# Windowed attention and a squared-ReLU feed-forward on one core: the second chunk of attention in plain float32, in another order of chunks

## The chip, the cores and the metric

One core of one Trainium2 chip runs the whole program. The metric is the time of one execution on the device in microseconds. Before the change it is 781.77 us (median of three runs, 781.71 to 782.03). Engines go by the profile's names: PE is the matrix engine, PEld its weight loads, DVE the vector engine, ACT the scalar engine, POOL the third elementwise engine, SP the queue that issues nearly all transfers.

## What is computed

```python
def _attn_ref(q, k, v, n_sink, window):          # q, k, v: [4, 8, 768, 64] float32
    scores = matmul(q, k.T) / sqrt(64)
    keep = (key < n_sink) | ((0 <= query - key) & (query - key < window))   # 4 and 128
    scores = where(keep, scores, -1e9)
    a = exp(scores - max(scores))
    return matmul(a / (sum(a) + 1e-9), v)

def _moe_ref(x, w_in, w_out, s, b):              # x: [3072, 512], w_in: [512, 2048]
    r = maximum(x @ w_in, 0)
    return (s * r * r + b) @ w_out
```

Inputs and output are float32. A second, general path in the program runs only if the limits on `n_sink` and `window` don't hold; with these inputs it is not taken.

## The kernel before

The 3072 rows are worked in eight **chunks** of 384 rows (`CH`), two per batch: an even chunk is the first half of a batch, an odd one the second half. Chunk *c* first gets its attention, which leaves its output transposed as two tiles `k.x[0]` and `k.x[1]` (a value rounded to the matrix engine's short float32 form, fp32r, and the remainder). Then the feed-forward of chunk *c* runs: 16 fragments *f* of the hidden width, each with a first product `h` (`l1`, 12 matmuls of 384 columns, L521) and a second product `po` (`l2`, 9 matmuls of 512 columns, L539), 32 steps in all. Both operands are split in two fp32r parts and three of the four partial products are added.

While the feed-forward of chunk *c* runs, the attention of chunk *c*+1 is put between its steps: the loop at L670 takes the feed-forward's steps one by one and, in proportion, the attention's slots. So there is a stretch with attention of chunk 0 alone, then seven **stages** (feed-forward of one chunk beside attention of the next), then the last feed-forward alone. A scheduler moves instructions within that order, engine by engine.

**Attention as in chunks 1 to 7** (`attn_slots`, L386) is split too. Per head, `prep_head` (L262) rounds queries, keys and values on ACT and forms the remainders on DVE (`qs`, L272) and POOL (`kl`, L273; `vv`, L278). A unit is one block of 128 queries: `unit_a` makes scores of at most 272 columns with two matmuls (L293, L294), masks and takes the row maximum on DVE (L298), exponentiates on ACT (L304) and copies the first keys' weights into `psk` on POOL (L305). `unit_b` transposes on PE, copies on ACT (L321), forms the remainder on DVE (`hl`, L322). `unit_c` multiplies by the values (L354), and per pair of heads `unit_d` adds what comes from the first keys and divides by the sum.

**Attention of chunk 0** (`first_slots`, L416) is plain: one float32 matmul per unit over all keys up to the diagonal (128, 256 and 384 columns, L443), mask and maximum (L445), exponent (L449), then `fn` divides by the row's sum on DVE (L460), `fb` transposes on PE (L468) and copies on ACT (L472), `fc` multiplies by the values (L480) in float32 into a bank of its own for each head, and casts and subtracts 64 partitions of it (L482, L483).

**The weights** come as 64-bit numbers. `make_weight` (L189) turns one fragment into two fp32r parts: two steps on ACT (L198, L199), two on DVE (L200, L201), an addition on POOL (L203), a cast on ACT (L208) and a subtraction on DVE or POOL (L214). `before(f)` calls it ahead of each `l1` of the first stage alone; the first two fragments are made during chunk 0's attention.

At the end, each feed-forward's three blocks of 128 rows are scaled by ACT into a tile `ot` (L543) and stored (L636). In the last one, all three take the two buffers of the tag `hl`.

Of the kernel before, what the change touches and what calls it, by code (L numbers as in the profile page):

```python
# [6 lines left out]
F32 = mybir.dt.float32  # L7
# [8 lines left out]
P = 128  # L16
# [17 lines left out]
E0, LB0, LC0 = 8, 4, 6  # L34
LB, LC, LD, L2 = 2, 4, 1, 2
# [3 lines left out]
def tile_kernel(ctx, tc, qT, kT, k0, v, vsk, n_sink, window, w, s, b, out):  # L39
# [15 lines left out]
    m_all = first.tile([P, 6 * P], MDT, tag="m", name="m_all")  # L55
# [34 lines left out]
    nc.sync.dma_start(lim[:, 0, :], n_sink.partition_broadcast(P))  # L90
    nc.sync.dma_start(lim[:, 1, :], window.partition_broadcast(P))
# [324 lines left out]
    def first_slots():  # L416
        k = Chunk()

        q = [wk.tile([P, NCC, CH], F32, tag=f"x{i}", name=f"q0{i}") for i in range(2)]
        k.x = [wk.tile([P, NCC, CH], F32R, tag=f"x{i}", name=f"x{i}_0") for i in range(2)]  # L420
        kk = first.tile([P, NCC, CH], F32, tag="k0", name="k0")
        vv = first.tile([P, NCC, CH], F32, tag="v0", name="v0")
        cc, tt, zz, sms = {}, {}, {}, {}

        def load():
            nc.gpsimd.memset(q[0][D:], 0.0)
            nc.vector.memset(q[1][:D], 0.0)
            for ps_ in (slice(0, 1), slice(1, NCC)):
                for hh in range(2):
                    hs = slice(hh * D, (hh + 1) * D)  # L430
                    nc.sync.dma_start(q[hh][hs, ps_, :], qT[0, ps_, hs, :CH].rearrange("r e s -> e r s"))
                    if hh == 0:
                        nc.sync.dma_start(kk[:, ps_, :], k0[:, ps_, :])
                nc.sync.dma_start(vv[:, ps_, :].rearrange("p r (n e) -> p r n e", n=BLK),
                                  v[0, ps_, :, :BLK].rearrange("r p n h d -> p r n (h d)"))

        def fa(h, i):
            pr = h // 2
            n = (i + 1) * P
            u = h * BLK + i  # L440
            uu = slice(u, u + 1)
            sc = psO.tile([P, 512], F32, tag="po", name="sc0")
            nc.tensor.matmul(sc[:, :n], q[h % 2][:, pr, i * P:(i + 1) * P], kk[:, pr, :n], start=True, stop=True)  # L443
            sm = first.tile([P, CH], F32, name="sm0", tag="sm0", bufs=E0)
            nc.vector.tensor_tensor_reduce(out=sm[:, :n], in0=sc[:, :n], in1=m_full[i], scale=-0.125, scalar=BIG,  # L445
                                           op0=ALU.add, op1=ALU.min, accum_out=negm[:, uu])
            if i == 0:
                zz[h] = first.tile([P, 2, BLK], F32, name="z0", tag="z0", bufs=4)
            nc.scalar.activation(sm[:, :n], sm[:, :n], AF.Exp, bias=negm[:, uu], scale=-1.0, accum_out=zz[h][:, 0, i:i + 1])  # L449
            sms[(h, i)] = sm  # L450

        def fn(h, i):
# [6 lines left out]
            sm = sms[(h, i)]  # L459
            nc.vector.tensor_scalar(out=sm[:, :n], in0=sm[:, :n], scalar1=z[:, 0, i:i + 1], scalar2=None, op0=ALU.mult)  # L460

        def fb(h, i):
            sm = sms.pop((h, i))
            if i == 0:
                tt[h] = first.tile([P, 4, 2 * P], F32, tag="tt0", name="tt0", bufs=3)
# [5 lines left out]
            out = tt[h][:, t0:t0 + i + 1, c0:c0 + P]  # L471
            nc.scalar.copy(out, tp[:, :(i + 1) * P].rearrange("p (k c) -> p k c", c=P))  # L472

        def fc(h):
            pr, hs = h // 2, slice(h % 2 * D, (h % 2 + 1) * D)
            o = ps("o0")
            t = tt.pop(h).rearrange("p k c -> p (k c)")
            for kb in range(BLK):
                c0 = kb * 3 * P
                nc.tensor.matmul(o[:, kb * P:CH], vv[:, pr, kb * P:(kb + 1) * P], t[:, c0:c0 + (BLK - kb) * P],  # L480
                                 start=(kb == 0), stop=(kb == BLK - 1))
# [4 lines left out]
        n = len(units)  # L486

        def slot(t):
            def f():
                if t == 0:  # L490
                    load()
                    constants()
                    nc.sync.dma_start(sb[:, 0:1], s.partition_broadcast(P))
                    nc.sync.dma_start(sb[:, 1:2], b.partition_broadcast(P))
                if t < n:
                    fa(*units[t])
# [4 lines left out]
                if 0 <= t - LB0 < n:  # L501
                    fb(*units[t - LB0])
                if 0 <= t - LC0 < n and (t - LC0) % BLK == BLK - 1:
                    fc((t - LC0) // BLK)
            return f

        return k, [slot(t) for t in range(n + LC0)]


    def moe_steps(x, store, wk, before=None, last=False):  # L510
# [21 lines left out]
        def l2(f):  # L532
            gg = g.pop(f)
            for tb in range(BLK):
# [6 lines left out]
                if f == NF - 1:  # L541
                    ot = wk.tile([P, DM], F32, name="ot", **(dict(tag="hl", bufs=HLB) if last else dict(tag="ot")))
# [115 lines left out]
    k, slots = first_slots()  # L658
# [86 lines left out]
```

## Time and profile before

| what | us |
|---|---|
| time, median of three runs | 781.77 |
| the profiled execution's own time | 781.77 |
| its span, first to last instruction | 780.0 |
| attention of chunk 0, from the first mask to the first `h` | 7.8 to 49.4 |
| first stage: feed-forward of chunk 0 beside attention of chunk 1 | 49.4 to 177.6 |
| second stage: feed-forward of chunk 1 beside attention of chunk 2 | 177.6 to 264.05 |
| third stage: feed-forward of chunk 2 beside attention of chunk 3 | 264.05 to 353.4 |
| last feed-forward alone | 705.1 to 772.5 |
| busy in the whole span: PE, DVE, ACT, POOL | 735.3, 513.6, 495.5, 268.8 |

The span is 1.8 us shorter than the time of the same execution. A stage is taken from the first `h` of one feed-forward to the first `h` of the next, as the chain of waits shows them. The granted clock is given as a share of the full one, 2.4 GHz; half of it is 1.2 GHz.

### The profile page before, as it was taken

The numbers are of one execution on the slowest core, as the hardware profiler recorded it, in microseconds if no ns is written. First come the engines' busy times: TensorE is split into PE (matmuls) and PEld (weight loads), VectorE is DVE, ScalarE is ACT, GpSimd is POOL, SyncE is SP. The second block draws the span as 40 slices with busy tenths as digits, with TensorE's granted clock in tenths as the row PEclk, the third lists the DMA queues.
The fourth block names the chain that finished last, engine by engine and source line by source line (L and its number), as shares of the span: only waits on it lengthen the run. The fifth ranks groups of instructions, "written<-read, shape, count | busy, mean of one in ns | idle before, by whom it ended". The sixth has DMA issues, their size and how long they took to land.

```text
span 780.0 us, 12112 instructions
## 1 busy us (share of the span) xinstructions
PE 735.3 (94%) x4036; PEld 656.9 (84%) x4036; DVE 513.6 (66%) x1250; ACT 495.5 (64%) x1231; POOL 268.8 (34%) x411
## 2 busy tenths in 40 slices
PE   7977988699999999999999999999999999999996
PEld 4655776579999999899999999899989999899985
DVE  6879998985676467655676466665676466663231
ACT  4886977766666576656666576656666576643222
POOL 3057668652343233322243233332343233210000
PEclk9989999999999999999999999999999999999998
DMA  7636205212112212112112212112111212001001
GB/s 271 273 103 229 105 14 170 76 34 77 42 54 59 73 43 67 35 43 76 43 53 57 76 43 62 40 43 76 43 53 55 77 43 60 21 1 42 1 1 45
DMA packets 28118, 54.21 MB, mean 70 GB/s; under 512 B 3600, under 2 KB 16528, under 8 KB 26128
## 3 DMA queue, kind: packets, MB, share of 16 engines
q1 hardware_dynamic: 28048, 53.36, 21.3%
q8 instruction: 34, 0.56, 0.3%
q14 instruction: 36, 0.29, 0.1%
HBM read 47.06 MB, written 6.29 MB: 68 GB/s over the span
## 4 chain that ended last, share of the span: by engine, by line
PE 76%; DVE 8%; ACT 7%; issue 3%; POOL 3%; DMA 2%; SPq 1%; ACTq 0%; POOLq 0%; DVEq 0%
PE h L521 30%; PE po L539 30%; PE o L354 5%; PE sc L294 2%; PE sc L293 2%; PE tp L317 2%; PE tp L316 2%; ACT w L199 1%; DVE r L525 1%; DMA w<-in_w 1%; PE o L480 1%; POOL w L203 1%; DVE w L201 1%; DVE qs L272 1%; ACT sm L304 1%
## 5 line engine op out<-in xcount | busy, mean ns | idle before, releaser
L521 PE MATMUL h<-x,w 128*128 128x384 f32 x1536 | 299.5, 343 | 8.7 <-DVE hl L322 3.8
L539 PE MATMUL po<-w,g 128*128 128x512 f32 x1152 | 301.6, 403 | 5.7 <-ACT g L527 3.7
L521 PEld LDWEIGHTS h<-x,w 128*128 128x128 f32 x1536 | 269.7, 190 | 14.5 <-issue 4.0
L539 PEld LDWEIGHTS po<-w,g 128*128 128x128 f32 x1152 | 211.6, 191 | 47.7 <-ACT g L527 4.9
L524 ACT ACTIVATE r<-h 128x384 f32<-128x384 f32 x128 | 62.9, 491 | 103.9 <-PE h L521 96.9
L298 DVE CUSTOM_DVE_ANT_0 sm<-sc,msk 128x272 f32<-128x272 f32 (+1 forms) x168 | 70.2, 418 | 78.4 <-PE sc L294 55.9
L525 DVE SCALAR_TENSOR_TENSOR r<-r,sb 128x384 f32<-128x384 f32 x128 | 84.1, 657 | 54.1 <-ACT r L524 54.0
L528 DVE SCALAR_TENSOR_TENSOR g<-r,sb,g 128x384 fp32r<-128x384 f32 x128 | 85.5, 668 | 45.6 <-ACT g L527 43.5
L305 POOL COPY psk<-sm 128x48 f32<-128x48 f32 x168 | 52.2, 311 | 162.9 <-ACT sm L304 161.7
L304 ACT ACTIVATE sm<-sm,negm 128x272 f32<-128x272 f32 (+1 forms) x168 | 85.4, 508 | 23.3 <-DVE negm L298 22.3
L527 ACT ACTIVATE g<-r,sb 128x384 fp32r<-128x384 f32 x128 | 78.7, 614 | 33.2 <-DVE r L525 32.1
L273 POOL TENSOR_TENSOR kl<-kraw,kh 128x544 fp32r<-128x544 f32 (+1 forms) x56 | 74.9, 1337 | 56.8 <-ACT kh L271 55.5
L321 ACT CAST hl<-tp 128x256 fp32r<-128x256 f32 (+1 forms) x168 | 58.8, 352 | 26.4 <-PE tp L317 26.2
L354 PE MATMUL o<-hl,vv 128*128 128x256 f32 (+1 forms) x400 | 71.4, 295 | 1.1 <-DVE hl L322 0.8
L322 DVE TENSOR_TENSOR hl<-tp,hl 128x256 fp32r<-128x256 f32 (+1 forms) x168 | 66.8, 398 | 7.5 <-ACT hl L321 6.7
L278 POOL TENSOR_TENSOR vv<-vraw,vv 128x256 fp32r<-128x256 f32 (+1 forms) x56 | 41.9, 747 | 60.9 <-ACT vv L277 59.0
L354 PEld LDWEIGHTS o<-hl,vv 128*128 128x128 f32 x400 | 54.9, 190 | 2.7 <-DVE hl L322 1.1
L293 PE MATMUL sc<-kh,qs 128*128 128x272 f32 (+1 forms) x168 | 47.8, 284 | 5.8 <-DVE hl L322 4.7
L363 DVE TENSOR_TENSOR xm<-o,y 64x384 f32<-64x384 f32 x56 | 31.0, 553 | 31.5 <-ACT y L362 31.3
L294 PE MATMUL sc<-kl,qs 128*128 128x272 f32 (+1 forms) x168 | 48.5, 289 | 0.0
L203 POOL TENSOR_TENSOR w<-w 128x1024 int32<-128x1024 int32 (+1 forms) x17 | 32.6, 1921 | 42.4 <-DVE z L458 19.3
L317 PE MATMUL tp<-identr,sm 128*128 128x128 f32 x168 | 45.7, 272 | 0.0
(112 smaller groups left out, 852.0 us busy)
## 6 DMA issues: line engine op xcount, KB each, us to landing
w<-in_w SPq DMA_DIRECT2D x15, 1024.0 KB, 8.9
kraw<-in_kT SPq DMA_DIRECT2D x32, 272.0 KB, 2.7
out<-ot SPq DMA_DIRECT2D x24, 256.0 KB, 2.0
qraw<-in_qT SPq DMA_DIRECT2D x28, 192.0 KB, 2.4
kraw<-in_kT SPq DMA_DIRECT2D x24, 208.0 KB, 2.4
vraw<-in_v SPq DMA_DIRECT2D x16, 256.0 KB, 2.7
vraw<-in_v SPq DMA_DIRECT2D x12, 192.0 KB, 2.3
vsraw<-in_vsk SPq DMA_DIRECT2D x28, 64.0 KB, 1.8
```

Source lines behind the costliest of these rows:

```text
L273: nc.gpsimd.tensor_tensor(out=hd.kl[:, :kw], in0=hd.k[:, :kw], in1=hd.kh[:, :kw].bitcast(F32), op=ALU.subtract)
L293: nc.tensor.matmul(sc[:, :n], hd.qs[:, qs], hd.kh[:, c0:c0 + n], start=True, stop=False)
L294: nc.tensor.matmul(sc[:, :n], hd.qs[:, qs], hd.kl[:, c0:c0 + n], start=False, stop=True)
L298: nc.vector.tensor_tensor_reduce(out=sm[:, :n], in0=sc[:, :n], in1=m, scale=-0.125, scalar=BIG, op0=ALU.add, op1=ALU.min, accum_out=negm[: ...
L304: nc.scalar.activation(sm[:, :n], sm[:, :n], AF.Exp, bias=negm[:, uu], scale=-1.0, accum_out=pp.zz[:, i, hh:hh + 1])
L322: nc.vector.tensor_tensor(out=lo, in0=tp[:, a:z], in1=hi.bitcast(F32), op=ALU.subtract)
L354: nc.tensor.matmul(hd.o[:, q0:q0 + n * P], hd.vv[:, kb, :], hd.hl[:, t, c0 * P:(c0 + n) * P], start=(hd.n == 0), stop=(i == BLK - 1 and kb ...
L521: nc.tensor.matmul(h[:, :CH], weight[f][:, 0, wi, cc * P:(cc + 1) * P], x[xi][:, cc, :], start=(i == 0), stop=(i == 11))
L525: nc.vector.scalar_tensor_tensor(out=r, in0=r, scalar=s_ap, in1=r, op0=ALU.mult, op1=ALU.mult)
L527: nc.scalar.activation(gg[:, 0, :], r, AF.Identity, bias=b_ap, scale=1.0)
L528: nc.vector.scalar_tensor_tensor(out=gg[:, 1, :], in0=r, scalar=b_ap, in1=gg[:, 0, :].bitcast(F32), op0=ALU.add, op1=ALU.subtract)
L539: nc.tensor.matmul(po[tb], gg[:, gi, tsl], weight[f][:, 1, wi, :], start=(f == 0 and i == 0), stop=(f == NF - 1 and i == 2))
```

## The change

It does four things.

- The chunks are worked in the order 0, 2, 1, 3, 4, 5, 6, 7, and chunk 2 (the first half of batch 1) gets its attention from the plain path, now `plain_slots(c)`, which the first stage holds. For chunk 2 its tiles come from the common pool under tags of the split path; its scores take a bank of the pool `psA`; per pair of heads `load_pair` loads keys, and per head queries and values beside 64 partitions or columns of zeros, which POOL writes.
- In both plain chunks the values of a head stand beside zeros, so that both heads of a pair add up in one bank, and one cast and one subtraction over 128 partitions take the place of two over 64.
- In chunk 0 the values are loaded head by head (8 transfers where there were 2), two of these and the two limits from ACT's queue; the mask tile moves to another pool.
- In the last feed-forward the third `ot` takes a buffer of the tag `ot`, so that each of the three has one of its own.

```diff
+ORDER = 0, 2, 1, 3, 4, 5, 6, 7
...
-    nc.sync.dma_start(lim[:, 0, :], n_sink.partition_broadcast(P))
-    nc.sync.dma_start(lim[:, 1, :], window.partition_broadcast(P))
+    nc.scalar.dma_start(lim[:, 0, :], n_sink.partition_broadcast(P))
+    nc.scalar.dma_start(lim[:, 1, :], window.partition_broadcast(P))
...
+                for pr in range(rs.start, rs.stop):
+                    for hh in range(2):
+                        hs = slice(hh * D, (hh + 1) * D)
+                        (nc.scalar if pr == 0 else nc.sync).dma_start(v0[:, pr, :, hh, hs], v[0, pr, :, :BLK, hh, :])
+
+        def zeros():
+            for hh in range(2):
+                nc.gpsimd.memset(v0[:, :, :, hh, (1 - hh) * D:(2 - hh) * D], 0.0)
+
+        def load_pair(pr):
+            kt = wk.tile([P, 544], F32, tag="kh", name="k_p")
+            nc.sync.dma_start(kt[:, :CH], k0[bb, :, pr, :])
+            for hh in range(2):
+                h = 2 * pr + hh
+                own, other = halves(h)
+                kk[h] = kt
+                q[h] = wk.tile([P, CH], F32, tag="qs", name="q_p")
+                nc.gpsimd.memset(q[h][other], 0.0)
+                nc.sync.dma_start(q[h][own], qT[bb, pr, own, :CH])
+                vv[h] = wk.tile([P, 4, P], F32, tag="vv", name="v_p", bufs=VB)
+                nc.gpsimd.memset(vv[h][:, :BLK, other], 0.0)
+                nc.sync.dma_start(vv[h][:, :BLK, own], v[bb, pr, :, :BLK, hh, :])
...
         def fc(h):
-            pr, hs = h // 2, slice(h % 2 * D, (h % 2 + 1) * D)
-            o = ps("o0")
+            pr, hh = h // 2, h % 2
+            if hh == 0:
+                os_[pr] = ps("o0")
+            o = os_[pr]
...
-                                 start=(kb == 0), stop=(kb == BLK - 1))
-            nc.scalar.copy(k.x[0][hs, pr, :], o[hs, :CH])
-            nc.vector.tensor_tensor(out=k.x[1][hs, pr, :], in0=o[hs, :CH], in1=k.x[0][hs, pr, :].bitcast(F32), op=ALU.subtract)
+                                 start=(hh == 0 and kb == 0), stop=(hh == 1 and kb == BLK - 1))
+            if hh == 1:
+                nc.scalar.copy(k.x[0][:, pr, :], o[:, :CH])
+                nc.vector.tensor_tensor(out=k.x[1][:, pr, :], in0=o[:, :CH], in1=k.x[0][:, pr, :].bitcast(F32), op=ALU.subtract)
...
-                    ot = wk.tile([P, DM], F32, name="ot", **(dict(tag="hl", bufs=HLB) if last else dict(tag="ot")))
+                    ot = wk.tile([P, DM], F32, name="ot", **(dict(tag="hl", bufs=HLB) if last and tb < 2 else dict(tag="ot")))
...
-    for c in range(NC_):
-        steps = moe_steps(k.x, store_at(c), wk, before if c == 0 else None, c == NC_ - 1)
+    for j, c in enumerate(ORDER):
+        steps = moe_steps(k.x, store_at(c), wk, before if j == 0 else None, j == NC_ - 1)
...
-            k, slots = attn_slots(c + 1)
+            k, slots = (plain_slots if j == 0 else attn_slots)(ORDER[j + 1])
```

Three places show what the scheduler made of it. The first is DVE in the first stage, between two fragments of weights. Before, the masks of the split path (L298) and the remainders `hl` stand between the weight steps L200, L201 and L214:

```order
L201 SCALAR_TENSOR_TENSOR w_456<-w_456,wt 128x1024
L528 SCALAR_TENSOR_TENSOR g<-r,sb,g 128x384
L322 TENSOR_TENSOR hl<-tp,hl 128x256
L298 ISA sm,negm<-sc,msk 128x272
L298 ISA negm 128x1
L322 TENSOR_TENSOR hl<-tp,hl 128x256
L200 TENSOR_SCALAR wt<-w_458 128x1024
L298 ISA sm,negm<-sc,msk 128x272
L298 ISA negm 128x1
L201 SCALAR_TENSOR_TENSOR w_458<-w_458,wt 128x1024
```

Now, with weight steps at L201, L202 and L215, the three divisions of a head (L497, of `sm_p`) stand together:

```order
L201 TENSOR_SCALAR wt<-w_460 128x1024
L576 SCALAR_TENSOR_TENSOR g<-r,sb,g 128x384
L495 RECIPROCAL z_p<-z_p 128x3
L202 SCALAR_TENSOR_TENSOR w_458<-w_458,wt 128x1024
L497 TENSOR_SCALAR sm_p<-sm_p,z_p 128x128
L497 TENSOR_SCALAR sm_p<-sm_p,z_p 128x256
L497 TENSOR_SCALAR sm_p_636<-sm_p_636,z_p 128x384
L215 TENSOR_TENSOR w_680<-w_456,w_680 128x2x512
L202 SCALAR_TENSOR_TENSOR w_460<-w_460,wt 128x1024
L201 TENSOR_SCALAR wt<-w_613 128x1024
```

The remainders `qs` and `hl` are gone from there, and the divisions are new. The second place is POOL in the first stage. Before, remainders and copies of the split path stand between the weights' additions (L203):

```order
L203 TENSOR_TENSOR w_261<-w_261 128x1024 [waits DVE_49]
L278 TENSOR_TENSOR vv<-vraw,vv 128x4x64 [waits Activation_49]
L305 COPY psk_95<-sm 128x3x16 [waits Activation_49]
L203 TENSOR_TENSOR w_263<-w_263 128x1024 [waits DMAHW7_49,DVE_49]
L273 TENSOR_TENSOR kl<-kraw,kh 128x544 [waits DMAHW2_49,Activation_49]
L305 COPY psk_95<-sm 128x3x16 [waits Activation_49]
L214 TENSOR_TENSOR w_638<-w_263,w_638 128x2x512 [waits Activation_49]
```

Now zeros for queries and values (L463, L466) stand there, and they wait for PE, which still reads the buffer that they fill:

```order
L463 MEMSET q_p 64x384 [waits DMAHW2_49,PE_49,Pool_49]
L215 TENSOR_TENSOR w_604<-w_269,w_604 128x2x512 [waits Activation_49,Pool_49]
L204 TENSOR_TENSOR w_456<-w_456 128x1024 [waits DMAHW6_49,DVE_49]
L204 TENSOR_TENSOR w_458<-w_458 128x1024 [waits DMAHW7_49,DVE_49]
L204 TENSOR_TENSOR w_460<-w_460 128x1024 [waits DMAHW0_49,DVE_49]
L463 MEMSET q_p 64x384 [waits DMAHW4_49,PE_49]
L204 TENSOR_TENSOR w_613<-w_613 128x1024 [waits DMAHW2_49,DVE_49,Activation_49]
L466 MEMSET v_p 128x3x64 [waits DMAHW3_49,PE_49]
```

So the additions for weights now stand in one queue behind steps of PE. The third place is ACT in chunk 0, where the first step on a weight, which waits for its transfer, stood as the 12th instruction after the cast of `sel`:

```order
L449 ACTIVATE sm_185,z_172<-sm_185,negm 128x384
L449 ACTIVATE sm_199,z_201<-sm_199,negm 128x128
L472 COPY tt_179<-tp_203 128x3x128
L449 ACTIVATE sm_210,z_201<-sm_210,negm 128x256
L198 ACTIVATE w_257<-w_257 128x1024
L472 COPY tt_213<-tp_214 128x128
```

It is now the 23rd, behind the fifth head's first exponent and the copies of three heads:

```order
L512 COPY tt_221<-tp_249 128x3x128
L512 COPY tt_259<-tp_260 128x128
L512 COPY tt_259<-tp_281 128x2x128
L512 COPY tt_259<-tp_296 128x3x128
L199 ACTIVATE w_263<-w_263 128x1024
L487 ACTIVATE sm_303,z_294<-sm_303,negm 128x256
```

That moves eleven instructions of attention ahead of that wait.

## Rows read from the trace of the kernel before

**Rows 1.** Stretches: length, busy PE, PEld, DVE, ACT, POOL (count), clock, DMA share, GB/s

```profile
7.80:49.40 41.60, 31.90 (x140) 22.03 (x139) 30.74 (x111) 33.79 (x92) 8.40 (x13) 0.90 0.59 232
49.40:177.60 128.20, 104.20 (x519) 86.81 (x519) 119.34 (x196) 99.88 (x201) 86.02 (x76) 0.94 0.33 112
177.60:264.05 86.45, 85.97 (x494) 79.22 (x493) 55.60 (x148) 55.86 (x152) 27.99 (x53) 1.00 0.19 55
264.05:353.40 89.35, 89.02 (x517) 82.24 (x517) 57.57 (x148) 58.28 (x152) 29.65 (x53) 1.00 0.18 55
```

**Rows 2.** First stage, groups by line and shape: busy us, mean ns, idle before

```profile
L528 DVE SCALAR_TENSOR_TENSOR g<-r,sb,g 128x384 fp32r<-128x384 f32 x16 | 16.0, 997 | 1.1 <-ACT g L527 1.1
L525 DVE SCALAR_TENSOR_TENSOR r<-r,sb 128x384 f32<-128x384 f32 x16 | 14.5, 903 | 0.0
L272 DVE TENSOR_TENSOR qs<-qraw,qs 64x384 fp32r<-64x384 f32 x9 | 12.1, 1343 | 0.3
L298 DVE CUSTOM_DVE_ANT_0 sm<-sc,msk 128x272 f32<-128x272 f32 x24 | 10.4, 432 | 0.5 <-PE sc L294 0.3
L322 DVE TENSOR_TENSOR hl<-tp,hl 128x256 fp32r<-128x256 f32 x24 | 9.9, 414 | 0.1
...
L273 POOL TENSOR_TENSOR kl<-kraw,kh 128x544 fp32r<-128x544 f32 x7 | 13.7, 1955 | 4.1 <-ACT kh L271 4.0
L305 POOL COPY psk<-sm 128x48 f32<-128x48 f32 x24 | 13.3, 559 | 4.6 <-ACT sm L304 4.5
```

**Rows 3.** Second stage, groups by line and shape

```profile
L525 DVE SCALAR_TENSOR_TENSOR r<-r,sb 128x384 f32<-128x384 f32 x16 | 10.0, 626 | 4.0 <-ACT r L524 4.0
L528 DVE SCALAR_TENSOR_TENSOR g<-r,sb,g 128x384 fp32r<-128x384 f32 x16 | 9.9, 617 | 5.5 <-ACT g L527 4.9
```

**Rows 4.** The chain of waits: start, us, what; float32 in chunk 0, then feed-forward

```profile
27.32 1.30 PE o L480 x6
28.62 0.33 PE tp L468 x3
...
182.31 2.12 PE h L521 x12
184.79 2.11 PE po L539 x9
```

**Rows 5.** Chunk 0 (7.5 to 49.4), groups by line

```profile
L449 ACT ACTIVATE sm<-sm,negm 128x128 f32<-128x128 f32 (+2 forms) x24 | 12.2, 508 | 3.7 <-DVE negm L445 3.6
L460 DVE TENSOR_SCALAR sm<-sm,z 128x128 f32<-128x128 f32 (+2 forms) x24 | 9.4, 447 | 0.1
L445 DVE CUSTOM_DVE_ANT_0 sm<-sc,m_all 128x128 f32<-128x128 f32 (+2 forms) x24 | 9.3, 417 | 1.6 <-PE sc L443 1.5
L472 ACT COPY tt<-tp 128x128 f32<-128x128 f32 (+2 forms) x24 | 8.5, 370 | 2.9 <-PE tp L468 2.6
...
L483 DVE TENSOR_TENSOR x<-o,x 64x384 fp32r<-64x384 f32 x7 | 3.9, 551 | 0.1
L482 ACT CAST x<-o 64x384 fp32r<-64x384 f32 x7 | 3.3, 473 | 1.0 <-PE o L480 0.9
```

**Rows 6.** Timeline of the start: the one large fill by POOL

```profile
0.90 1.37 POOL L426 MEMSET q<- 64x1536 f32 x1
```

**Rows 7.** Timeline of chunk 0, DVE's divisions and POOL: start, us, engine, line

```profile
29.20 1.90 POOL L203 TENSOR_TENSOR w<-w 128x1024 int32<-128x1024 int32 x1 [19.27 <-DVE z L458]
...
29.42 2.35 DVE L460 TENSOR_SCALAR sm<-sm,z 128x128 f32<-128x128 f32 x3
...
33.11 0.86 DVE L460 TENSOR_SCALAR sm<-sm,z 128x128 f32<-128x128 f32 x3
```

**Rows 8.** Chunk 0's first weight: the chain of waits, then the timeline

```profile
7.80 8.88 DMA w<-in_w
...
16.70 1.10 ACT L198 ACTIVATE w<-w 128x1024 int32<-128x1024 uint32 x1 [2.94 <-DMA w<-in_w]
```

**Rows 9.** Timeline of the end, the third block's scaling

```profile
773.92 0.60 ACT L543 ACTIVATE ot<-po 128x512 f32<-128x512 f32 x1 [1.46 <-DMA out<-ot]
```

More of the change, by code (lines that the diff above doesn't have):

```diff
@@ L413, in attn_slots, with plain_slots, halves, load_all @@
         return k, [slot(t) for t in range(n + LC + LD)]
-    def first_slots():
+    def plain_slots(c):
         k = Chunk()
[L419 to L428, printed above, removed]
+        k.c, bb = c, c // 2
+        q, kk, vv, cc, tt, zz, os_ = {}, {}, {}, {}, {}, {}, {}
+        if c == 0:
+            q0 = [wk.tile([P, NCC, CH], F32, tag=f"x{i}", name=f"q0{i}") for i in range(2)]
+            k0_ = first.tile([P, NCC, CH], F32, tag="k0", name="k0")
+            v0 = first.tile([P, NCC, BLK, 2, P], F32, tag="v0", name="v0")
+            for h in range(H):
+                q[h] = q0[h % 2][:, h // 2, :]
+                kk[h] = k0_[:, h // 2, :]
+                vv[h] = v0[:, h // 2, :, h % 2, :]
+        k.x = [wk.tile([P, NCC, CH], F32R, tag=f"x{i}", name=f"x{i}_{c}") for i in range(2)]
+        def halves(h):
+            own, other = slice(0, D), slice(D, P)
+            return (own, other) if h % 2 == 0 else (other, own)
+        def load_all():
+            nc.gpsimd.memset(q0[0][D:], 0.0)
+            nc.vector.memset(q0[1][:D], 0.0)
+            for rs in (slice(0, 1), slice(1, NCC)):
@@ L437, in fa @@
         def fa(h, i):
-            pr = h // 2
             n = (i + 1) * P
-            u = h * BLK + i
+            u = (c * H + h) * BLK + i
             uu = slice(u, u + 1)
-            sc = psO.tile([P, 512], F32, tag="po", name="sc0")
-            nc.tensor.matmul(sc[:, :n], q[h % 2][:, pr, i * P:(i + 1) * P], kk[:, pr, :n], start=True, stop=True)
-            sm = first.tile([P, CH], F32, name="sm0", tag="sm0", bufs=E0)
+            sc = psO.tile([P, 512], F32, tag="po", name="sc0") if c == 0 else ps("sc0")
@@ L445, in fa @@
+            nc.tensor.matmul(sc[:, :n], q[h][:, i * P:(i + 1) * P], kk[h][:, :n], start=True, stop=True)
+            if c == 0:
+                sm = first.tile([P, CH], F32, name="sm0", tag="sm0", bufs=E0)
+            elif i < 2:
+                sm = wk.tile([P, W], F32, name="sm_p", tag="sm", bufs=SMB)
+            else:
+                sm = wk.tile([P, 544], F32, name="sm_p2", tag="kl")
             nc.vector.tensor_tensor_reduce(out=sm[:, :n], in0=sc[:, :n], in1=m_full[i], scale=-0.125, scalar=BIG,
@@ L500, in f @@
                         fn(t // BLK, i)
[L501 to L504, printed above, removed]
+                if 0 <= t - lb < n:
+                    fb(*units[t - lb])
+                if 0 <= t - lc < n and (t - lc) % BLK == BLK - 1:
+                    fc((t - lc) // BLK)
             return f
-        return k, [slot(t) for t in range(n + LC0)]
+        return k, [slot(t) for t in range(n + lc)]
     def moe_steps(x, store, wk, before=None, last=False):
```

47 lines of the change are left out of this document (27 added, 20 removed).

## The prediction

> **What bounds the kernel now.** I read the share of busy time first (PE 94% of the span), then cut the span at the places where one feed-forward's first `h` follows another's, and read the busy time of each engine per stretch [rows 1]. The reader is to see that the 94% hides two regimes. From 177.6 us on, PE is busy to within half a microsecond of each stage (85.97 of 86.45, 89.02 of 89.35) at the full clock: there only PE's work counts. In the first stage, 49.4 to 177.6, it is another engine: DVE is busy 119.34 of 128.20 us (93%), ACT 99.88, POOL 86.02, and PE's clock falls to 0.94 of full on average because PE waits. The same feed-forward beside the same kind of attention takes 89.35 us later, so this one stage holds some 39 us that PE does not need. Chunk 0's attention before it (41.6 us) is bound by no single engine: 31.9, 30.7 and 33.8 us on PE, DVE and ACT.
>
> Next I read the first stage by groups [rows 2]. DVE does three things there: the weights, the squares `r` and `g` (14.5 + 16.0 us), and the attention of chunk 1, of which `qs`, the masks and `hl` alone are 12.1 + 10.4 + 9.9 us. The same `r` and `g` cost 626 and 617 ns each in the second stage [rows 3] and 903 and 997 ns here; the difference goes with POOL, which is busy two thirds of this stage and one third of the next.
>
> **The first stage, PE's side.** Plain float32 costs PE more. Three products of 384, 256 and 128 columns (six records) took 1.30 us and three transposes 0.33 us back to back [rows 4]. A head needs two such sets of products and six transposes: 2 x 1.30 + 2 x 0.33 = 3.26 us, a chunk 8 x 3.26 = 26.1 us. The feed-forward is 16 x 2.12 + 16 x 2.11 = 67.7 us [rows 4]. So PE needs 93.8 us in the changed stage, where the split path beside the same feed-forward needed 89.35 [rows 1]: 4.4 us more work.
>
> **The first stage, DVE's side.** Off go the groups above (32.4 us) and some 17 us in smaller groups of the same attention, which I estimate by the second half's usual stage: it has 57.57 us of DVE in all [rows 1], less 16 x (0.626 + 0.617) = 19.9 for the squares, so attention is 37.7 even where POOL does not disturb, and the 12.1 us of `qs` here would there be about 5. I take 37.7 as the lower and 49 as the upper end. On come the plain groups as chunk 0 shows them: masks 9.3, divisions 9.4, subtractions 4 x 0.55 [rows 5], and about 5 us of the short steps of sums and maxima: 26 us. DVE then stands at 119.3 - 49 + 26 = 96 to 119.3 - 38 + 26 = 107 us if its other work stays as dear as now. It should not: POOL loses `kl` and `psk` (13.7 + 13.3 us [rows 2]) and more, and gets 16 fills of a quarter of the size that took 1.37 us [rows 6] or less, some 5 us. If the squares came down to their price of the second stage, that is 30.5 - 19.9 = 10.6 us less. So DVE lies between 85 and 107 us; with POOL's load about halved I take 93. ACT loses the roundings of queries, keys and values, keeps exponents (12.2) and copies of transposes (8.5 [rows 5]); from 99.9 it falls, and binds less than now.
>
> **Its length.** PE at 93.8 and DVE near 93 leave no cover for each other's waits. For how near a stage comes to its busiest engine there are two rows: 93% in this stage now, with one clear bound, and 33.79 of 41.60 = 81% in chunk 0, where three engines are level [rows 1]. So 93.8/0.93 = 101 to 93.8/0.81 = 116 us. I take 106.5 (88%), nearer the first, because the weights' chain, the order of the stage and its length are those of this stage. That is 128.2 - 106.5 = 21.7 us less (27 to 12).
>
> A rule speaks against this part. Three divisions of one head took 2.35 us beside an addition of POOL and 0.86 us without one [rows 7]; eight heads bring 24 of them into the stage where POOL adds the weights. The Trainium skill says in "SBUF — State Buffer", section "Who interferes with whom", that a DVE instruction of the copy or tensor-scalar kind can take both ports, one pair of which is POOL's, and that the later of the two then waits for the whole instruction of the other. By that rule every head could lose what this one lost, and the trace agrees in the one place shown. I price it from the rows: 8 x (2.35 - 0.86) = 12 us at most, if each head meets an addition. POOL will be busy about half the stage, so half of it, 6 us, is in the 93 above already; all of it makes a rival below.
>
> **The stage after.** The second stage now carries attention of chunk 1, a second half, instead of chunk 2, a first half. Both prices are in [rows 1]: 89.35 - 86.45 = 2.9 us dearer. All later stages keep their kinds. +2.9.
>
> **Chunk 0.** ACT's first step on a weight waited 2.94 us for its transfer, which took 8.88 us from its issue at 7.80 [rows 8]. In the new order eleven more instructions of attention stand ahead of it, over 4 us of work at 508 and 370 ns [rows 5], so the wait should be covered. Twelve issues stood ahead of that transfer on SP, which came at 7.80, so at most 0.65 us each; now fourteen do, so it lands up to 1.3 us later. Four casts and four subtractions go: 4 x 0.473 on ACT and 4 x 0.551 on DVE [rows 5]. POOL's two fills beside the values, 1.37 us together by [rows 6], find room, since it is busy 8.40 of the 41.6 us [rows 1]. Bounds: -4.5 us (wait and casts both gone) and +1.3 (the wait merely moves). I take -2.5.
>
> The values now come in pieces of 64 numbers, 256 bytes, where a pair's 128 numbers stood together. "DMA: Bandwidth & Descriptors", section "Specifications", of the Trainium skill says that pieces under 512 bytes don't reach full rate; no row here has such a transfer of this size. By it chunk 0's term would be nearer to 0 than to -2.5, an estimate.
>
> **The end.** The third block's scaling waited 1.46 us for the first block's store [rows 9]; its new buffer was last stored a stage earlier. The last store follows it directly: -1.5.
>
> **The sum** is made against the profiled execution's 781.77, which is also the median: -21.7 + 2.9 - 2.5 - 1.5 = -22.8, **759.0 us**. With all the ends: -27.3 + 2.9 - 4.5 - 1.5 = -30.4, 751.4; and -12.4 + 2.9 + 1.3 - 1.5 = -9.7, 772.1.
>
> **Rivals.**
> - *PE fills up at once.* If DVE falls to 85 us, PE alone binds as in the later stages: 93.8 plus some 3 us at the start, 97. -31.2 + 2.9 - 2.5 - 1.5 = -32.3: 749.5. For it: later stages lose half a microsecond. Against it: their DVE is at 57 us, not 85. Chance 0.10.
> - *DVE stays the bound.* The rule above: all heads meet POOL, DVE is at 93 + 6 = 99 to 107, at 88% of the stage 113 to 121; take 117. -11.2 + 2.9 - 2.5 - 1.5 = -12.3: 769.5. For it: 997 [rows 2] against 617 ns [rows 3]. Against it: POOL's smaller load. Chance 0.14.
> - *POOL closes a ring, and it gets slower.* Twelve of the sixteen fills wait until PE has read the buffer's last use, and the weights' additions stand behind them in the same queue; PE waits for those weights. Where PE reaches a fill's release just before it needs the next weight, the addition, the cast and the subtraction are on its path. One such passage is POOL 1.9 us [rows 7] and more for the cast and the remainder. From the forecast to no gain it takes 22.8/12 = 1.9 us at each fill, which is one addition per fill; all twelve with 2.1 us, a step of the feed-forward [rows 4], give 759 + 25 = 784. For it: the order puts fills directly ahead of additions. Against it: in the order the weights' additions stand two or three fragments ahead of PE. Chance 0.05, of which 0.04 ends slower.
> - That the change does not do what it says is excluded for its main part by the order: the divisions and no `qs` or `hl` stand in the first stage.
>
> **How the numbers follow.** My forecast has 0.70, the floor 0.10, DVE 0.14, the ring 0.05, and 0.01 is left for a stall in no row. The range 750 to 772 takes in the forecast's ends and the DVE rival and leaves out most of the floor and the ring: about 8 in 10. A change is told from none at 0.2%, 1.6 us. Faster is forecast, floor and DVE: 0.94. Slower is the ring's 0.04; the rest of the ring and the unknown stall are the same, 0.02.
>
> **What would show it.** The stretch from the first `h` to the second feed-forward's first `h` should be 101 to 116 us, with PE busy above 95% of it, the clock above 0.97 and `r` and `g` near 750 ns. The next stage should be 89.4 us. The first `h` should come at about 47 us, and ACT's wait for the first weight be under 1 us. The last scaling should wait for PE alone. I am wrong if DVE is still over 93% busy in the first stage, if PE waits there for POOL's products, or if the second stage is longer than 90 us.

## The result and the profile after

The changed kernel takes 776.38 us (median of 4 runs, 776.11 to 776.96), the kernel before 781.74 beside it (4 runs): a ratio of 0.9934, 95% interval 0.9920 to 0.9947. It is faster, but by 5.4 us and not by the 22.8 forecast, and it lies outside the range. The profiled execution took 776.96 us.

The same stretches as in [rows 1], for the changed kernel (length; busy PE, PEld, DVE, ACT, POOL; clock; DMA share; GB/s):

```profile
7.80:42.50 34.70, 26.47 (x135) 18.66 (x134) 29.32 (x116) 29.80 (x84) 6.43 (x13) 1.00 0.93 296
42.50:169.90 127.40, 105.32 (x488) 84.85 (x487) 103.67 (x173) 83.65 (x166) 52.00 (x38) 0.95 0.27 93
169.90:259.30 89.40, 89.10 (x518) 82.27 (x517) 57.60 (x148) 58.07 (x151) 29.79 (x52) 1.00 0.21 61
```

Chunk 0 is 6.9 us shorter (41.60 before), the second stage 2.95 longer, and the first stage, where 21.7 us were to go, lost 0.8. DVE did lose its work there (119.34 to 103.67) and POOL too (86.02 to 52.00). The time did not follow. The sum of the three, -6.9 - 0.8 + 2.95, is the change of the span, 780.0 to 775.2, to within 0.1 us.

The groups of that stage that answer to [rows 2] (line, operation, tiles, shapes, count | busy us, mean ns | idle before):

```profile
L573 DVE SCALAR_TENSOR_TENSOR r<-r,sb 128x384 f32<-128x384 f32 x16 | 19.9, 1241 | 4.3 <-ACT r L572 4.3
L576 DVE SCALAR_TENSOR_TENSOR g<-r,sb,g 128x384 fp32r<-128x384 f32 x16 | 12.7, 792 | 3.2 <-ACT g L575 3.1
L204 POOL TENSOR_TENSOR w<-w 128x1024 int32<-128x1024 int32 x11 | 24.1, 2196 | 32.8 <-DVE w L202 24.7 <-ACT tt_p L512 5.5 <-ACT sm_p L487 2.5
L497 DVE TENSOR_SCALAR sm_p<-sm_p,z_p 128x256 f32<-128x256 f32 x8 | 6.1, 761 | 0.0
L494 DVE TENSOR_SCALAR z_p<-z_p 128x3 f32<-128x3 f32 x8 | 5.5, 691 | 0.5 <-ACT sm_p L487 0.5
```

`r`, which was to fall from 903 to about 750 ns, rose to 1241. A step `z_p` on three columns takes 691 ns on average. The timeline shows why (start us, us, engine, line, operation):

```profile
70.24 2.28 POOL L204 TENSOR_TENSOR w<-w 128x1024 int32<-128x1024 int32 x1 [2.83 <-DVE w L202]
70.69 2.24 DVE L573 SCALAR_TENSOR_TENSOR r<-r,sb 128x384 f32<-128x384 f32 x1
...
75.73 0.62 DVE L573 SCALAR_TENSOR_TENSOR r<-r,sb 128x384 f32<-128x384 f32 x1
...
89.89 2.20 POOL L204 TENSOR_TENSOR w<-w 128x1024 int32<-128x1024 int32 x1 [1.16 <-DVE w L202]
90.26 1.86 DVE L494 TENSOR_SCALAR z_p<-z_p 128x3 f32<-128x3 f32 x1
```

The `r` that starts 0.45 us after a POOL addition ends 0.41 us after that addition does; the next one, alone, takes 0.62. The `z_p` ends 0.03 us after its addition.

Not every DVE step is held. The masks (L481) take scores from a bank that PE wrote, and one tile; one that ran at 78.72, inside the addition from 78.41 to 80.56, took its 0.41 us. The steps of `L202` or `L215` beside such an operation took up to 2.57 us, alone 1.2.

The same stage in pieces, in the columns of [rows 1]:

```profile
60.00:80.00 20.00, 15.89 (x77) 12.46 (x78) 20.00 (x36) 15.00 (x28) 7.93 (x5) 1.00 0.27 106
80.00:104.00 24.00, 18.95 (x83) 15.39 (x82) 23.85 (x33) 16.64 (x30) 11.82 (x9) 0.86 0.08 21
104.00:116.00 12.00, 8.54 (x41) 6.18 (x39) 9.07 (x10) 4.31 (x10) 7.38 (x5) 1.00 0.58 194
116.00:145.00 29.00, 23.57 (x118) 19.03 (x117) 26.10 (x59) 22.21 (x53) 11.37 (x11) 1.00 0.17 50
145.00:170.00 25.00, 24.38 (x115) 20.90 (x116) 9.94 (x22) 10.79 (x26) 4.48 (x5) 0.93 0.12 35
```

DVE's 81% of the stage is a mean of two parts. From 60 to 104 us it is busy 43.85 of 44 us and PE 34.84; from 145 us on, when the weights are made, PE is busy 24.38 of 25 and DVE 9.94.

### The profile page after: what moved, and what is told of

The parts are those of the page before. It is cut to its first block, busy times and chain, and to the rows that moved or that the text cites. A ratio compares the mean times of both kernels' runs of the same rounds, so it can differ in the third digit from the quotient of the medians.

```text
span 775.2 us, 11989 instructions
## 1 busy us (share of the span) xinstructions
PE 733.9 (95%) x4024; PEld 654.1 (84%) x4024; DVE 497.0 (64%) x1222; ACT 477.8 (62%) x1187; POOL 237.1 (31%) x377
## 4 chain that ended last, share of the span: by engine, by line
PE 78%; DVE 9%; ACT 3%; issue 2%; POOL 1%; DMA 1%; ACTq 0%; DVEq 0%; POOLq 0%
PE h L569 32%; PE po L587 30%; PE o L355 5%; PE sc L295 2%; PE sc L294 2%; PE tp L318 2%; DVE w L202 2%; PE tp L317 2%; DVE r L573 1%; DVE w L215 1%; DVE wt L201 1%; DVE sm_p L497 1%; DVE g L576 1%; PE o L522 1%; PE ts L368 1%
## 5 line engine op out<-in xcount | busy, mean ns | idle before, releaser
L572 ACT ACTIVATE r<-h 128x384 f32<-128x384 f32 x128 | 62.9, 492 | 114.3 <-PE h L569 110.2
L299 DVE CUSTOM_DVE_ANT_0 sm<-sc,msk 128x272 f32<-128x272 f32 (+1 forms) x144 | 60.8, 422 | 80.4 <-PE sc L295 65.6
L306 POOL COPY psk<-sm 128x48 f32<-128x48 f32 x144 | 38.3, 266 | 166.0 <-ACT sm L305 164.7
L305 ACT ACTIVATE sm<-sm,negm 128x272 f32<-128x272 f32 (+1 forms) x144 | 73.7, 512 | 20.4 <-DVE negm L299 19.2
L274 POOL TENSOR_TENSOR kl<-kraw,kh 128x544 fp32r<-128x544 f32 (+1 forms) x48 | 61.4, 1279 | 56.3 <-ACT kh L272 50.0
L322 ACT CAST hl<-tp 128x256 fp32r<-128x256 f32 (+1 forms) x144 | 51.3, 356 | 28.7 <-PE tp L318 28.2
L323 DVE TENSOR_TENSOR hl<-tp,hl 128x256 fp32r<-128x256 f32 (+1 forms) x144 | 57.9, 402 | 8.1 <-ACT hl L322 7.2
L355 PE MATMUL o<-hl,vv 128*128 128x256 f32 (+1 forms) x352 | 61.5, 293 | 0.0
L279 POOL TENSOR_TENSOR vv<-vraw,vv 128x256 fp32r<-128x256 f32 (+1 forms) x48 | 34.8, 724 | 59.8 <-ACT vv L278 57.4
L295 PE MATMUL sc<-kl,qs 128*128 128x272 f32 (+1 forms) x144 | 41.4, 287 | 0.0
L294 PE MATMUL sc<-kh,qs 128*128 128x272 f32 (+1 forms) x144 | 40.4, 281 | 0.0
```

The lines of the kernel that those rows point to most:

```text
L274: nc.gpsimd.tensor_tensor(out=hd.kl[:, :kw], in0=hd.k[:, :kw], in1=hd.kh[:, :kw].bitcast(F32), op=ALU.subtract)
L295: nc.tensor.matmul(sc[:, :n], hd.qs[:, qs], hd.kl[:, c0:c0 + n], start=False, stop=True)
L323: nc.vector.tensor_tensor(out=lo, in0=tp[:, a:z], in1=hi.bitcast(F32), op=ALU.subtract)
L355: nc.tensor.matmul(hd.o[:, q0:q0 + n * P], hd.vv[:, kb, :], hd.hl[:, t, c0 * P:(c0 + n) * P], start=(hd.n == 0), stop=(i == BLK - 1 and kb ...
L572: nc.scalar.activation(r, h[:, :CH], AF.Relu, scale=1.0 / WUP)
```

## Experiments

Theory 1: POOL's operations that read two tiles, the weights' additions above all, hold DVE off, and the weights' preparation keeps the first stage long. Rivals: late transfers of weights (2), POOL's fills that wait for PE ahead of its additions (3), attention left over behind the last weight (4). In each run I read where the second stage's first `h` comes: 177.6 us before, 169.9 after.

**The two parts apart.** The first keeps the new first chunk alone, the second the float32 half alone.

```diff
-ORDER = 0, 2, 1, 3, 4, 5, 6, 7
+ORDER = 0, 1, 2, 3, 4, 5, 6, 7
-            k, slots = (plain_slots if j == 0 else attn_slots)(ORDER[j + 1])
+            k, slots = attn_slots(ORDER[j + 1])
```

> The changed kernel with the old order of chunks and with the split attention in the first stage again: only the new first chunk and the buffers of the last stores are left of the change. If the whole gain of 5.4 us is the first chunk's (first h at 42.5 instead of 49.4 us) and the float32 half is worth nothing in the first stage (128.2 to 127.4) and costs 2.9 in the second, this kernel takes 781.7 - 6.9 = 774.8 us, 1.5 below the changed one. If instead the late first weight of the new first chunk (issued at 14.75 instead of 7.80 us) was paid for in the first stage, that stage is longer than 128.2 us here and the time is 777 to 782.

```diff
-            v0 = first.tile([P, NCC, BLK, 2, P], F32, tag="v0", name="v0")
+            v0 = first.tile([P, NCC, CH], F32, tag="v0", name="v0")
...
-            if hh == 0:
-                os_[pr] = ps("o0")
+            if hh == 0 or c == 0:
+                os_[pr] = ps("o0")
...
+            if c == 0:
+                hs = slice(hh * D, (hh + 1) * D)
+                nc.scalar.copy(k.x[0][hs, pr, :], o[hs, :CH])
```

> The changed kernel with the old first chunk (values of both heads in one tile, two accumulations a pair, small loads and the first weight as before): only the float32 half in the first stage is left. If the two parts add up, first h is back at 49.4, the first stage is 127.4 and the second 89.4 us, and the time is 776.4 + 6.9 = 783.3 us, slower than before by 1.5. If the new first chunk spoiled the first stage (late weights, the sub-512-byte pieces of its loads), the stage is 107 to 115 us here and the time 764 to 771.

The first chunk alone: 782.15 us, ratio 1.0005 (0.9994 to 1.0015), no gain. The float32 half alone: 779.23, ratio 0.9969 (0.9957 to 0.9981). The stretches of the first, then those of the second:

```profile
7.80:42.10 34.30, 26.04 (x132) 18.43 (x132) 29.31 (x115) 29.63 (x86) 6.13 (x11) 1.00 0.87 281
42.10:177.05 134.95, 106.72 (x526) 91.11 (x525) 122.04 (x197) 101.11 (x205) 88.58 (x77) 0.91 0.31 107
```

```profile
7.80:49.30 41.50, 31.35 (x140) 21.52 (x139) 30.89 (x113) 33.81 (x90) 5.68 (x10) 0.92 0.68 246
49.30:173.50 124.20, 105.78 (x484) 87.11 (x483) 103.35 (x173) 83.16 (x164) 51.26 (x38) 0.92 0.27 96
```

The first `h` came 7.3 us earlier in the first run, and the stage became 6.8 us longer: its end stayed (177.05 against 177.6). DVE's work over both stretches is 29.31 + 122.04 = 151.35 us, before 30.74 + 119.34 = 150.08. The time and the longer stage are what the expectation gave for a late first weight, but no step of ACT or DVE waited for a weight's transfer in either stretch. I read it so: with split attention DVE's work sets the end of the stage, wherever its first `h` lies. The float32 half alone brought the end forward by 4.1 us and paid 2.9 back in the second stage. Both together brought it forward by 7.7: with less work for DVE the earlier start is worth something.

**The stage without attention, and without POOL's additions.**

```diff
+        if c:
+            def fill():
+                for x in k.x:
+                    nc.gpsimd.memset(x.bitcast(F32), 0.0)
...
+            return k, [fill]
...
         return k, [slot(t) for t in range(n + lc)]
```

> The changed kernel with no attention at all in the first stage: the rows of chunk 2 are filled with zeros and not computed (its output rows are wrong by that much), so that the stage holds only the weights' preparation and 16 steps of MoE. PE has 67.7 us of work there. Theory 1 (the weights' preparation is paced by DVE and POOL, which hold each other up on the same memory port, and attention adds to that): the stage falls to 75 to 95 us. Theory 2 (the transfers of the weights set the pace): it stays above 100 us, with the waits before the first step on a weight ended by DMA. Theory 4 (attention left over behind the last weight is the tail): stage 85 to 103 us.

```diff
-                nc.gpsimd.tensor_tensor(out=hi, in0=hi, in1=lo, op=ALU.add)
```

> The changed kernel without POOL's integer addition of the weights' low bits (the three lowest bits of each weight are left out). It takes 17 of POOL's operations, some 34 us of its 52, out of the first stage; nothing is put in their place. Theory 1 (port held by POOL blocks DVE): DVE's r falls from 1241 to under 900 ns, its busy time in the stage from 104 to 80-88 us and the stage from 127.4 to 107-118 us. Theory 2 or 4 (transfers, or attention left over for PE): r falls too, but the stage moves by under 4 us.

Without attention the stage still takes 101.5 us for 67.7 us of feed-forward (752.84 us in all, a single run). By its number that spoke for late transfers, and it lies in theory 4's range as well. But no step of PE, DVE, ACT or POOL waited for a transfer in that stage, and DVE's rows point elsewhere: one-input shifts of the weights (`L201`), which no attention stands beside, took 1403 ns there and 688 without the additions. Without the additions the time is 754.2 us, ratio 0.9649 (0.9629 to 0.9669), and the stage 108.35, 19 us less with the attention untouched, as theory 1 gave it; theories 2 and 4 gave under 4:

```profile
7.80:38.50 30.70, 25.71 (x133) 18.50 (x132) 25.15 (x113) 26.93 (x82) 2.65 (x11) 1.00 1.00 316
38.50:146.85 108.35, 99.51 (x490) 82.18 (x489) 86.89 (x174) 84.90 (x169) 18.64 (x21) 0.98 0.33 115
```

`r` fell only to 1099 ns, where theory 1 gave under 900. Its five longest, 1.39 to 2.77 us, each start within 0.5 us of one of POOL's remaining two-input operations.

**Load or place in the chain?** An addition can cost by holding DVE off, or because each weight's cast waits for it. In the next run POOL adds as before, but into a scratch tile that no step reads.

```diff
-                nc.gpsimd.tensor_tensor(out=hi, in0=hi, in1=lo, op=ALU.add)
+                nc.gpsimd.tensor_tensor(out=t, in0=hi, in1=lo, op=ALU.add)
```

> The changed kernel in which POOL makes every addition as before, but writes the sum to the scratch tile that nobody reads: the weights go on without it (their three lowest bits are left out). POOL's load and whatever it holds up on the port stay, its place in the chain from weight to weight goes. If the additions cost by holding DVE off the port, DVE's r stays at 1150 to 1250 ns, the stage above 120 us and the time at 770 to 777. If they cost by their own 2.2 us and their waits in the chain ACT, DVE, POOL, ACT, POOL or DVE of each weight, the stage is 108 to 114 us and the time 754 to 761. Between these, each has its share.

777.77 us, ratio 0.9948 (0.9934 to 0.9961): nothing gained over the changed kernel, though the list of waits of this stage has no step of ACT, DVE or PE that waited for an addition (ACT's casts waited 6.5 us for them in the changed kernel).

```profile
40.20:170.85 130.65, 107.71 (x490) 88.35 (x489) 103.06 (x174) 86.63 (x169) 49.65 (x38) 0.92 0.26 91
```

Against the run without additions, DVE has the same 174 instructions and 103.06 instead of 86.89 us. The place in the chain costs nothing that can be seen here; the load does. Now POOL is nearly as busy at the same place (46.66 us in the stage, 49.65 with the sum aside), but only writes:

```diff
-                nc.gpsimd.tensor_tensor(out=hi, in0=hi, in1=lo, op=ALU.add)
+                for _ in range(2):
+                    nc.gpsimd.memset(t, 0)
```

> The changed kernel with two fills of the scratch tile by POOL in the place of each addition (the three lowest bits of the weights are left out): POOL is as long busy at the same places of its queue and writes the tile that the sum went to in the run with the sum aside (777.8 us), but reads nothing. If it is POOL's reading beside DVE's operations with two inputs that costs, DVE's r falls to 620-900 ns and the stage to 108-115 us: 754 to 762 us. If POOL's place in the queues or any use of its port costs, r stays above 1050 ns and the time above 768. The Trainium skill's page SBUF — State Buffer (Who interferes with whom) says that an operation of DVE with two inputs meets only a POOL operation that reads; by it the first holds for r, while DVE's copies and scalings with one input, which it counts among those that take both ports, would still be held up.

763.65 us, ratio 0.9783 (0.9755 to 0.9810); stage 114.1 us. The expectation doesn't decide: the stage lies in the range given for reading, `r`'s mean of 1065 ns in that given for any use of what POOL shares with DVE, and the time between the two. The timeline does (lines of other work between are left out):

```profile
64.74 0.96 POOL L205 MEMSET wt<- 128x1024 int32 x1 [3.46 <-DVE w L202]
...
64.95 0.07 DVE L482 DVE_READ_ACCUMULATOR2_ANT negm<- 128x1 f32 x1
64.95 0.61 DVE L574 SCALAR_TENSOR_TENSOR r<-r,sb 128x384 f32<-128x384 f32 x1
...
75.59 2.84 POOL L216 TENSOR_TENSOR w<-w,w 128x1024 fp32r<-128x1024 f32 x1 [2.08 <-ACT w L210]
...
76.04 2.80 DVE L574 SCALAR_TENSOR_TENSOR r<-r,sb 128x384 f32<-128x384 f32 x1
```

Beside a fill `r` takes its 0.61 us; all four above 0.9 us stand beside POOL's remaining two-input operations, such as this subtraction. So it is POOL's reading that stops `r`. The fills still cost 9.4 us over no addition at all, and there it was mostly DVE's one-input steps that grew (divisions of 256 columns: 676 ns, without additions 346; shifts `L201` of 1024: 839 against 688). The Trainium skill's page "SBUF — State Buffer", section "Who interferes with whom", says that a DVE instruction with two inputs in SBUF contends with a POOL instruction that reads SBUF, not with one that only writes it, and that copies and scalings can contend in a mode that takes both of DVE's pairs of ports. The trace agrees with both: 0.61 us beside a fill and 2.80 beside the subtraction, and 676 ns beside fills. The prediction had used only what bears on steps of the second kind, and `r` is of the first.

**The rivals.** Without fills (whole rows of both heads loaded in their place), and with chunk 2's 20 transfers on POOL's queue instead of SP's:

```diff
-                nc.gpsimd.memset(q[h][other], 0.0)
-                nc.sync.dma_start(q[h][own], qT[bb, pr, own, :CH])
+                nc.sync.dma_start(q[h], qT[bb, pr, :, :CH])
...
```

> The changed kernel without POOL's fills in the first stage: the queries and values of chunk 2 are loaded in whole rows, both heads of a pair, by the same transfers, so that nothing has to be filled with zeros (each head's scores and products then hold the other head's as well: that part of the computation is changed). Rival 3 (POOL's additions stand behind fills that wait for PE to free a buffer): the stage falls from 127.4 to 110-118 us and the time to 760-767. Theory 1 (additions and DVE hold each other off the port): the stage stays at 124 to 129 us and the time at 773 to 778.

```diff
-                nc.sync.dma_start(q[h][own], qT[bb, pr, own, :CH])
+                nc.gpsimd.dma_start(q[h][own], qT[bb, pr, own, :CH])
...
```

> The changed kernel with the 20 transfers of chunk 2's keys, queries and values on POOL's queue instead of SP's, where they stood ahead of the weights' transfers. Theory 2 (late weights set the stage: 4.7 us of the chain before 109 us lay in a transfer of weights issued late): the stage falls by 4 to 8 us and the time to 768-772. Theory 1: within 1.5 us of 776.4, or slower where POOL's own issuing delays its additions.

777.98 us (774.89 to 778.39) without fills, the stage 127.55: the ring of fills costs nothing that can be seen. 779.17 us (ratio 0.9963, 0.9951 to 0.9975) with the transfers moved, the stage 127.1. That run is not clean: POOL spent 9.2 us of the stage on the issues, and the time came 2.8 us above the changed kernel's. But SP no longer waited behind chunk 2's loads, and its weights' transfers then waited for DVE's step `L202`, 56.0 us in one wait: the last transfer of that line (L172) was issued by 110.2 us, in the changed kernel by 109.5. So late transfers look like an effect of slow preparation, not its cause.

**Was the float32 half worth anything?** The kernel before, without its additions (`L203`):

```diff
-                nc.gpsimd.tensor_tensor(out=hi, in0=hi, in1=lo, op=ALU.add)
```

> The kernel before, with split attention in the first stage, without POOL's additions (the three lowest bits of the weights are left out). If the additions were the bound that hid the float32 half's worth, this kernel keeps a DVE-bound stage: DVE 119 less the 17 us that it fell in the changed kernel is 102, over 0.93 is 110 us, plus an earlier first h (45 to 47): 759 to 766 us, 5 to 12 above the changed kernel without additions. If the additions alone set the stage in both kernels, it is at 752 to 757, no slower than the changed kernel without them.

767.79 us, ratio 0.9812 (0.9795 to 0.9829), 1.8 above the range of the first case. The changed kernel without additions takes 754.2: without them the change is worth 13.6 us (12.7 by the two ratios), with them 5.4.

```profile
48.20:163.65 115.45, 97.76 (x519) 83.22 (x519) 105.89 (x196) 98.10 (x201) 54.97 (x59) 0.96 0.37 124
```

Here DVE is busy 92% of the stage, in the changed kernel without additions 80% and PE 92%: by these mean shares the bound passed from DVE to PE, as forecast, once POOL let it. It is a close thing: until 123 us, while weights are still made, the changed kernel without additions has DVE busy 76.5 and PE 76.7 of 84.5 us.

**The end.** The flag is computed ahead of the last chunk's feed-forward:

```diff
+        if j == NC_ - 1:
+            bad = const.tile([P, 4], F32, tag="bad", name="bad")
...
+            nc.vector.tensor_copy(flag, cnt[0:1, 0:1])
         steps = moe_steps(k.x, store_at(c), wk, before if j == 0 else None, j == NC_ - 1)
...
-    bad = const.tile([P, 4], F32, tag="bad", name="bad")
...
-    nc.vector.tensor_copy(flag, cnt[0:1, 0:1])
```

> The changed kernel with the check of its inputs (the reductions, the small matmul and the flag, L740 to L742) computed ahead of the last chunk's MoE instead of behind it; only the register load and the branch stay at the end. If the 7.36 us from the flag to the end of the span is the flag's way (load into registers, branch), they now start earlier and the end lies nearer to the last store: 772 to 775 us. If that stretch is the last stores' landing and the program's end, nothing moves: 776 us within 0.7.

775.62 us (774.57 to 777.51), ratio 0.9927 (0.9913 to 0.9941): the interval overlaps the changed kernel's. The traces separate it better. The last stores of the changed kernel and its flag, then the flag of the kernel before:

```profile
766.34 1.98 ACT L591 ACTIVATE ot<-po 128x512 f32<-128x512 f32 x3 [3.03 <-PE po L587]
766.96 1.71 SPq L684 DMA_DIRECT2D out<-ot  x3
...
767.84 0.15 DVE L742 CAST flag<-cnt 1x1 int32<-1x1 f32 x1 [3.87 <-PE cnt L740]
```

```profile
772.67 0.15 DVE L694 CAST flag<-cnt 1x1 int32<-1x1 f32 x1 [3.88 <-PE cnt L692]
```

From the start of the flag's cast to the span's end it is 780.0 - 772.67 = 7.33 us before and 775.2 - 767.84 = 7.36 now, though the last scaling ended 5.5 us from the end before and 6.9 now. From the start of the stores' issues to the span's end it is 775.2 - 766.96 = 8.24 us; with the early flag 773.9 - 767.12 = 6.78. So in these traces about 1.5 us of the end were the flag's path, and the last store was not what ended the span.

**A version that beats both.** The low bits go in by an `or` within DVE's shift (ACT's step rounds down so that nothing carries); then also the weights' last subtractions on DVE, and the early flag.

```diff
-                nc.scalar.activation(lo, lo.bitcast(U32), AF.Copy, scale=2.0 ** -29)
+                nc.scalar.activation(lo, lo.bitcast(U32), AF.Copy, bias=-0.5, scale=2.0 ** -29)
-                nc.vector.tensor_scalar(out=t, in0=hi, scalar1=3, scalar2=None, op0=ALU.logical_shift_left)
+                nc.vector.scalar_tensor_tensor(out=t, in0=hi, scalar=3, in1=lo, op0=ALU.logical_shift_left, op1=ALU.bitwise_or)
-                nc.gpsimd.tensor_tensor(out=hi, in0=hi, in1=lo, op=ALU.add)
```

> The changed kernel with the low bits put in by a bitwise or on DVE, inside the shift that is there already (its ACT step rounds down, so that nothing has to carry): POOL's 17 additions are gone and nothing of the computation is left out. Against the run without additions (754.2) it gives 15 of DVE's shifts a second input. If one DVE step with two inputs costs what L202 does (1.2 against 0.7 us), that is 17 x 0.5 = 8 us more of DVE in a stage in which DVE was busy 87 of 108 us: PE-bound still, 754 to 757 us. If DVE is at its limit there, 758 to 764.

```diff
...
-                e = nc.gpsimd if f % 4 == 3 else nc.vector
+                e = nc.vector
...
```

> The changed kernel with the low bits put in by DVE's bitwise or (756.1 us alone), with the 4 of 16 remaining subtractions of the weights that POOL still made (2.6 to 3.0 us each) on DVE, and with the flag computed ahead of the last chunk. In the run with the or alone three of DVE's operations beside these subtractions took 2.1 to 2.7 us instead of 0.6. Theory 1: the stage falls by 1 to 4 us from 109.9, and the early flag gives 1.3: 751 to 755 us. If DVE is the limit there (93 of 110 us busy): 755 to 757.

756.13 us (ratio 0.9671, 0.9656 to 0.9686) and 748.94 (0.9591, 0.9571 to 0.9611). The first stage of the second:

```profile
39.40:142.25 102.85, 97.32 (x489) 81.37 (x488) 88.65 (x179) 83.19 (x167) 8.43 (x16) 1.00 0.34 119
```

Its `r` in the groups of that stretch:

```profile
L572 DVE SCALAR_TENSOR_TENSOR r<-r,sb 128x384 f32<-128x384 f32 x16 | 10.7, 670 | 5.5 <-ACT r L571 5.5
```

DVE took on all that POOL did for the weights and is busy 15 us less than in the changed kernel. PE is busy 95% of the stage at the full clock. The subtractions' move and the flag brought 7.2 us (6.3 by the two ratios), more than the 2 to 5 expected; the stage gave 7.05 of it. DVE makes five more subtractions there than with the `or` alone and is busy 4.3 us less (92.97 to 88.65).

## Why the prediction was wrong

- **The first stage, DVE's side: this step failed.** I let the squares fall toward their later price because "POOL's load [is] about halved", and put "half of it, 6 us, in the 93 above". POOL's load did fall, by 34 us, but that was attention's; the weights' 17 additions and 5 subtractions, which read two tiles and take 1.9 to 3.3 us each (some half as long), stayed. Beside 20 of these 22 the timeline has a DVE step, or a head's three divisions, that is longer than alone. DVE came to 103.67 us, inside my 85 to 107 but near the wrong end. What stalled was not the 24 divisions alone, which I priced at 12 us at most: against the last run, where POOL has no such operation for the weights, `r`, which I took to get cheaper, is 9.2 us dearer, the divisions 5.3, the short step `z_p` 4.2 and `g` 2.3.
- **Its length: failed with it.** "PE at 93.8" over 88% let PE's total set the length and took the two engines as level. The changed stage is 127.4 us. From 60 to 145 us DVE is busy 79.0 of 85 us, until 104 almost without a gap, with PE behind it; then PE alone works off what was left (24.4 us busy of 25). The sign that I had named, DVE over 93% busy, did not show because I had tied it to the mean of the whole stage, 81%; nor did a wait of PE for POOL. With the additions gone, 108.35 us lies within the 101 to 116 of this step, and with the subtractions gone 102.85.
- **PE's side: short.** 93.8 us were counted; PE is busy 97.3 in the run where its clock is full (1.00), and 105.3 in the changed stage at 0.95.
- **The rival "DVE stays the bound" had the mechanism and a price too small.** It gave 113 to 121 us for the stage and 769.5 in all; measured are 127.4 and 776.38.
- **The second stage: right.** 89.40 us for 89.35.
- **Chunk 0: the step failed in its addition.** The first `h` came 6.9 us earlier, more than the 2.5 taken, and ACT's wait for the first weight is gone. But that gain alone moved nothing (1.0005): I added a start to a stage whose end, as I read it, DVE's work sets. That 6.9 lies outside my bounds has a part in PE's clock, for which I had no term. It was granted 0.90 of full over chunk 0 before and 1.00 after. Before, PE waited 8.4 us for divisions there, was busy 1.54 of 5 us from 38 to 43, and from 43 to 49.4 the clock was 0.59, so mostly at the lower level of 1.2 GHz; the chain has three sets of six products at 2.55, 2.00 and 2.94 us, 3.6 us more than three at the 1.30 of [rows 4]:

```profile
38.00:43.00 5.00, 1.54 (x9) 1.04 (x7) 4.54 (x10) 4.70 (x8) 1.90 (x1) 1.00 0.00 0
43.00:49.40 6.40, 5.77 (x18) 4.08 (x19) 2.83 (x5) 5.09 (x10) 2.73 (x3) 0.59 0.04 10
```

```profile
20.33 2.55 PE o L480 x6
...
43.67 2.00 PE o L480 x6
...
46.88 2.94 PE o L480 x6
```

  No run takes the clock apart from the rest. The issue of the first weight was misjudged too: "fourteen at most 0.65 us" gave 1.3 us later; it came at 14.75 instead of 7.80:

```profile
5.72 7.99 SPq L449 DMA_DIRECT2D v<-in_v  x6
...
14.75 1.67 SPq L172 DMA_DIRECT2D w<-in_w  x3
```

  Six transfers in 256-byte pieces took 8 us to issue. It cost nothing visible: no step of ACT waited for a weight's transfer.
- **The end: wrong.** 1.5 us forecast. The third scaling does wait for PE alone now, but the end came no earlier: by the traces the flag's path ends the span, not the last store.
- **The ring: rightly held small.** Without fills the stage keeps its length (127.55 us).

The direction was right, but by luck in its parts: the stage that was to bring 21.7 us brought 0.8, and the start that was to bring 2.5 brought 6.9, which without the float32 half is worth nothing.

Open: how the 22 us of stage between the run with the sum aside and the run without it split between DVE's 16 us of longer steps and the waits behind them; how much of chunk 0's gain is PE's clock; and why moving the weights' last subtractions (three, and two of half the size) brought 7 us.

## What to carry to other kernels

Before an engine's relief is turned into time, look for what makes its instructions long: if a small instruction's mean in one stage is well above that in another, find the neighbour in the timeline that it ends with, and ask whether the change removes that neighbour. Read busy shares piece by piece: here a mean of 81% hid 44 us in which DVE was hardly ever free. Taking two fifths off POOL's load gave DVE's `r` no relief while the long operations that read two tiles remained; a step that costs DVE 0.5 us more can be cheaper there than 2.2 us of POOL beside it. And a part that starts a stage earlier is worth something only if the stage's end depends on its start.

## What the runs showed of the hardware

Not expected: that a three-column DVE step can take 1.86 us beside a POOL addition (0.16 without additions), while masks kept their time inside one (0.41 us); that a POOL fill leaves `r` (two inputs) at 0.61 us while it stretches one-input divisions from 346 to 676 ns; and that 6.8 us lie between the start of the last stores' issues and the end of the span even when no flag is computed there.
